# First stage of a tuned Fourier-mixing kernel by even and odd parts: 24x24 matrices on sixteen 32x32 tiles in place of 47x48 matrices on four 64x64 tiles

## The chip, the cores and the metric

The kernel runs on one core of a Trainium2 chip. A core has five engines with instruction queues of their own: TensorE (PE: matrix products; PEld is its loading of the stationary matrix), VectorE (DVE), ScalarE (ACT), GpSimd (POOL) and SyncE (SP, used here only to start DMAs). Matrix products are written to PSUM, eight banks of 2 KB for each of 128 partitions; everything else lies in SBUF. The metric is the device time of one execution in microseconds. Everything is float32.

## The reference

The input `x` has 8 batches of 3008 tokens by 256 channels. Each batch is Fourier transformed along its tokens, multiplied by a filter, and transformed back; the 24064 tokens then go through a feed-forward layer of width 2048 with a hard swish.

```python
X = np.fft.rfft(x, axis=1)
y = np.fft.irfft(X * (filt_r + 1j * filt_i)[None], n=3008, axis=1)
t = y.reshape(24064, 256)
h = t @ w_in                                  # 256 -> 2048
out = (h * np.clip(h + 3.0, 0.0, 6.0) / 6.0) @ w_out
```

## The kernel before

**The feed-forward layer** is the main loop. The 24064 tokens are 47 blocks of 512, and the 2048 hidden channels 8 parts of 256, so that there are 376 steps, block by block and part by part. Both products of a step are done with seven half-size products in place of eight (Strassen's scheme). A step's seven "up" products (A11, S1, A12, S2, S4, S3, A22; functions `up_1` to `up_5`) alternate between the two PSUM tiles `al` and `be`; its seven "down" products (`down`, numbered 1 to 7, always for the step before) go to four banks `po`. Between them ACT copies (L779, L780, L789, L808) and takes relu (L813), DVE adds (L794, L799), takes the hard swish (L818, twice a step, called half 0 and half 1 here) and makes the sums that Strassen's scheme needs (L825, L826, L831). Every float32 product is two passes over the array; a matrix with 64 output columns takes half of the array, so that `strips` sends each product as two halves that run side by side. The other inputs of a block, sums of its tokens, are made on POOL by `t_sums` (L760), once a block.

**The Fourier part** is threaded between these steps. 3008 = 47 x 64, and the transform of a batch goes in stages: the *first stage* transforms along the 47 (frequency index k, 24 of them), for each of 64 offsets c; its result goes through DRAM (`z_tmp`); the *second stage* (`b_unit`) transforms along c; then the filter (`f_unit`, `y_unit` on DVE), the way back (`bi3_unit`, result through DRAM as `g_tmp`), and last `n_five`/`n_unit`, which make the feed-forward layer's input in the ring `xn`, from which `t_sums` reads. PSUM tiles of the Fourier part are two, `psf`, used in turn by all these units; `be` is borrowed at some places.

**The first stage before.** For batches 2 to 7 (counted from 0) `a6_unit` takes 6 offsets at a time of each half of c (six units in a batch, the last with 2). For each offset it multiplies 47 rows of x by a matrix of 48 columns that holds cosines, sines and the turning factors (twiddles) of this offset; the matrices of all 32 offsets lie in `wa`. Four such products run side by side on 64x64 tiles of the array. The halves of c (h = 0, 1) land in two `psf` tiles and `be`; ACT copies one half to SBUF, and `a6_sums` on DVE makes the sum and difference of both. `z6_store` starts four DMAs from POOL's queue. A unit's x comes with four DMAs from SP (`x_load`).

**What sets the order.** Each engine's order is written out by hand: `plan` maps a step and a place in it to calls (`at`). Place 0 is after the first up products, place 1 before A22, place 2 at the end of the step. `A_AT` holds the steps of the first-stage units, counted from 7 blocks before the batch's first block; `places` those of the other stages. `late(i)` puts L831 of a step after L799 where DVE had much to do in the step before (`HEAVY`). A step that has no unit of the Fourier part is called plain below.

```python
up_1: A11 -> al, S1, A12 -> be; ACT copies al and be
do(0); DVE: hard swish half 1, L825, L826; down 1
up_2: S2 -> al, S4 -> be; DVE L794; down 2, 4
up_3: S3 -> al; DVE L799; down 5, 6; ACT relu; do(1); DVE: hard swish half 0
up_5: A22 -> al; ACT L808, relu; down 7, 3; do(2)
```

Of the kernel before, what the change touches and what calls it, by code (L numbers as in the profile page):

```python
# [10 lines left out]
FP32 = mybir.dt.float32  # L11
I32 = mybir.dt.int32
AXT = mybir.ActivationFunctionType
ALU = mybir.AluOpType
# [27 lines left out]
SIX = tuple(range(0, HC, 6))  # L42
# [36 lines left out]
def _make_tables():  # L79
# [17 lines left out]
    wf = np.zeros((P, 4, 64))  # L97
    re, im = slice(0, NC), slice(NC, P)
# [10 lines left out]
    for q in range(64):  # L109
        g, sign = (q, 1.0) if q < 32 else (31 - q, -1.0)  # L110
        co, si = (f([2 * np.pi * ((j * g) % NC) / NC for j in range(HC + 1)]) for f in (np.cos, np.sin))
        ab = np.concatenate([co, np.zeros(HC - 1) if q == 63 else si[1:HC]])
        cd, dc = ab * np.where(np.arange(NC) > HC, -1.0, 1.0), np.roll(ab, HC)
        wi[q, 3], wi[HALF + q, 3] = cd, sign * dc

        at = g % 2 * 32 + (q // 2 if q < 32 else 16 + (q - 32) // 2)
        wi[at, 0], wi[HALF + at, 0] = cd, sign * dc
        cs, sn = (np.array([f(2 * np.pi * ((j * g) % NC) / NC) for j in range(HC)]) for f in (np.cos, np.sin))
        if g % 32 == 0:
            sn = np.zeros(HC)  # L120
        for r in range(0, P, HALF):
            wf[r:r + 32, g % 2, at % 32], wf[r + 32:r + 64, g % 2, at % 32] = cs, sn
            wf[r:r + 32, g % 2, 32 + at % 32], wf[r + 32:r + 64, g % 2, 32 + at % 32] = -sign * sn, sign * cs

        for h in range(2):
            s = -1.0 if h and g % 2 else 1.0
            wf[h:HALF:2, 2, at], wf[HALF + h::2, 2, at] = s * cs, s * sn
            wf[h:HALF:2, 3, at], wf[HALF + h::2, 3, at] = -s * sign * sn, s * sign * cs
        wi[q, 1], wi[HALF + q, 1] = cd, -cd
        wi[q, 2], wi[HALF + q, 2] = sign * dc, sign * dc  # L130
# [49 lines left out]
    return wa.astype(f), wai.astype(f), wb.astype(f), wi.astype(f), wf.astype(f), start.astype(f), direct.astype(f)  # L180
# [3 lines left out]
def kernel(  # L184
# [11 lines left out]
    wa_np, wai_np, wb_np, wi_np, wf_np, start_np, direct_np = _make_tables()  # L196
# [4 lines left out]
    wf_d = nc.inline_tensor(wf_np, name="wf_t").ap()  # L201
    start_d = nc.inline_tensor(start_np, name="start_t").ap()
# [5 lines left out]

    o_d = nc.dram_tensor("o_tmp", (B * HC * NA, D), FP32, kind="Internal").ap()
# [173 lines left out]
    def x_at(b, c):  # L383
        if b == 1:
            return xs[:, (b * NB + c) % 3, :, :], c * XC, XC
        t = xs.rearrange("p i j d -> p (i j) d")
        return t[:, ds((b * len(SIX) + c) % 2 * 6, 6), :], SIX[c], min(6, HC - SIX[c])

    def x_load(b, c):
        t, c0, n_ = x_at(b, c)  # L390
        rows = x[b].rearrange("(a c) d -> a c d", c=NC)
        for h in range(2):
            for r, n in ((0, 32), (32, NA - 32)):
                nc.sync.dma_start(t[h * 64 + r:h * 64 + r + n, 0:n_, :], rows[r:r + n, ds(h * HC + c0, n_), :])

# [70 lines left out]
    def a6_unit(b, c):  # L470
        xc, c0, n = x_at(b, c)
        n //= 2
        t = t3p.tile([P, 3, 2, D], FP32, name="t3") if n == 3 else t1p.tile([P, 2, 2, D], FP32, name="t1")
        banks = [psF.tile([P, 512], FP32, name="psf", tag="f") for h in range(2)]
        be = psU.tile([P, 512], FP32, name="be") if n == 3 else None
        for r in range(n):
            for g in range(2):
                for h in range(2):
                    j, ps, o = (2, be, h) if r == 2 - 2 * h and n == 3 else (r - h if n == 3 else 0,) + (banks[h], r - h if n == 3 else 0)
                    q = g * n + j  # L480
                    nc.tensor.matmul(ps[ts(g, 64), ts(o, D)], wa[ds(h * 64, NA), ds((c0 + q) * 2 * KH, 64)],  # L481
                                     xc[ds(h * 64, NA), q, :], start=True, stop=True)
            if n == 3 and r == 0:
                nc.vector.tensor_copy(out=t[:, 2, 1, 0:2], in_=be[:, D:D + 2])
        m = min(n, 2)
        two = [ps[:, 0:m * D].rearrange("p (j d) -> p j d", d=D) for ps in banks]
        nc.scalar.activation(out=t[:, 0:m, 0, :], in_=two[0], func=AXT.Copy)
        if n == 3:
                nc.scalar.activation(out=t[:, 2, 1, 2:D], in_=be[:, D + 2:], func=AXT.Copy)
        st["t1", b, c] = t, be, two[1], n  # L490

    def a6_sums(b, c):
        t, be, ps, n = st["t1", b, c]
        v, m = nc.vector, min(n, 2)
        if n == 3:
            v.tensor_tensor(out=t[:, 2, 0, :], in0=be[:, 0:D], in1=t[:, 2, 1, :], op=ALU.add)
            v.tensor_tensor(out=t[:, 2, 1, :], in0=be[:, 0:D], in1=t[:, 2, 1, :], op=ALU.subtract)
        v.tensor_tensor(out=t[:, 0:m, 1, :], in0=t[:, 0:m, 0, :], in1=ps, op=ALU.subtract)
        v.tensor_tensor(out=t[:, 0:m, 0, :], in0=t[:, 0:m, 0, :], in1=ps, op=ALU.add)

    def z6_store(b, c):
        t, _, _, n = st.pop(("t1", b, c))
        for g in range(2):
            for ri in range(2):
                p0 = g * 64 + ri * KH
                nc.gpsimd.dma_start(z_d[b, :, ri, ds(SIX[c] + n * g, n), :, :].rearrange("k j s d -> k (j s d)"),  # L506
                                    t[p0:p0 + KH, 0:n, :, :].rearrange("p j s d -> p (j s d)"))
# [24 lines left out]
    def b_unit(b, i):  # L532
        c, r = divmod(2 * i, TC)
        if b > 1:
            t = st.pop(("t2", b, c))
            ps = [bank(b) for k in range(2)]
            for s_ in range(2):
                for ri in range(2):
                    for k in range(2):
                        nc.tensor.matmul(ps[k][ds(ri * 64 + s_ * 32, 32)].rearrange("p (v d) -> p v d", v=2),  # L540
                                         wf[ts(k, 64), s_, ts(ri, 32)], t[ts(k, 64), :, s_, :], start=True, stop=True)
            for k in range(2):
                st["ps", b, i + k] = ps[k].rearrange("p (u d) -> p u d", u=2)
            return
        ps = bank(b).rearrange("p (u d) -> p u d", u=2)
        for u in range(2):

            k, w = (r // 2 + 2 * u, wf[:, 2:4, :].rearrange("p a m -> p (a m)")) if b else (r + u, st["wb", b, c][:, r + u, :])
            (strips if b else nc.tensor.matmul)(ps[:, u, :], w, st["t2", b, c][:, k, :], start=True, stop=True)
        st["ps", b, i] = ps  # L550
# [219 lines left out]
    def up_1(k, p):  # L770
# [5 lines left out]
        product(al, p, A11, t[:, F1, :], start=True)  # L776
        product(be[:, 1, :], p, S1, xb(k, 0, 1), start=True)
# [197 lines left out]
    EARLY = (a_unit, b_unit, bi_unit, n_unit, n_five)  # L975

    def at(step, fn, *a):
        plan.setdefault((step, 0 if fn in EARLY else 1 if fn in (w_scale, bi3_unit, a6_unit) else 2), []).append((fn, a))

    with tc.manual_schedule():  # L980
# [120 lines left out]
        at(0, wai_load)  # L1101
        at(2, x_load, 1, 2)
# [37 lines left out]
        A_AT = (4, 6, 10, 12, 14, 15)  # L1140

        def places(n):
# [4 lines left out]
            a_at = [k - 7 * NP + i for i in A_AT]  # L1147
# [7 lines left out]
        for n in range(1, B):  # L1155
            a_at, f_at, y_at, bi_at = places(n)
            for c, s in enumerate(a_at):
                at(s, a_unit if n == 1 else a6_unit, n, c)
                at(s, a_sums if n == 1 else a6_sums, n, c)
                at(s, *((z_store, n, c, nc.sync) if n == 1 else (z6_store, n, c)))  # L1160
                if c >= (3 if n == 1 else 2):
                    at(max(a_at[c - 3 + (n > 1)], s - 6), x_load, n, c)
                elif n > 1:
                    at(max(prev[-1 if n == 2 else c - 2], s - 6), x_load, n, c)
            for c in range(NT):
                s = f_at[2 * (c - TB) + (n == 1)] + 1 if c >= TB else a_at[-1] + 1
                at(s, t2_load, n, c)
                s = f_at[2 * (c - FB) + 1] + 1 if c >= FB else a_at[-1 if n > 1 else 3] + 1
                at(s, table_load, n, c)
# [13 lines left out]
        HEAVY = (f_unit, y_unit, a_sums, n_five, a6_sums, bi3_unit)  # L1183

        def late(i):
            return i % NP in (1, 2) or any(fn in HEAVY for place in range(3) for fn, a in plan.get((i - 1, place), ()))

        items = [(k, p) for k in range(NBLK) for p in range(NP)]
        for i in range(len(items) + 1):
# [19 lines left out]
            up_1(k, p)  # L1209
            ends = k == LAST and p == NP - 1  # L1210
            do(0)
            last_plain = dn and kd == 0
            dn = dn and kd > 0
            if dn:
# [10 lines left out]
            if dn:  # L1225
                down(kd, pd, 2, 4)
# [26 lines left out]
            if dn:  # L1253
                if pd == NP - 1 or ends:
                    out_2(kd)
                down(kd, pd, 7, 3)
# [33 lines left out]
```

## Time and profile before

| | |
|---|---|
| median of 3 runs | 2608.41 us (2608.24 to 2608.5) |
| the profiled execution | 2608.8 us, span 2607.0 us, TensorE clock 1.0 |
| PE / PEld busy | 2591.8 us (99%) / 2051.0 us (79%) |
| DVE / ACT / POOL busy | 2053.9 us (79%) / 1295.6 us (50%) / 486.7 us (19%) |
| DMA | 200.32 MB, mean 77 GB/s |

A line of a group says: source line, engine, operation, the tile written and the tiles read, partitions x elements, how often, and then the busy time in us and the mean of one in ns. A line of the timeline says: start in us, length in us, engine, line, operation, tiles, shapes, count of merged instructions, and in square brackets the idle time of the engine ahead of it and who ended it. A float32 matrix product shows as two MATMUL instructions, one for each pass, so that the two halves of an up product are four.

### The profile page before, as it was taken

What the parts mean: (1) busy time and instruction counts of PE and PEld (TensorE: products, weight loads), DVE (VectorE), ACT (ScalarE), POOL (GpSimd) and SP (SyncE); (2) the same over time, 40 slices, a digit from 0 to 9 for tenths busy, and PEclk for the clock granted to TensorE, in tenths of its full rate; (3) what the DMA queues carried; (4) which work ended last, traced back from release to release, by engine and by line L of the source; (5) the groups of instructions that cost most, each with busy time, mean ns of one, the idle gap of its engine ahead of it and who ended that gap; (6) DMA issues with size and microseconds to landing.
All of it is one profiled execution on the core that took longest, in us unless ns stands there. A gap on an engine that the chain in (4) does not pass through costs nothing.

```text
span 2607.0 us, 86613 instructions
## 1 busy us (share of the span) xinstructions
PE 2591.8 (99%) x37708; PEld 2051.0 (79%) x37708; DVE 2053.9 (79%) x3611; ACT 1295.6 (50%) x2677; POOL 486.7 (19%) x711
## 2 busy tenths in 40 slices
PE   8999999999999999999999999999999999999999
PEld 6487777878778787788877888777877778888887
DVE  7978868888788877888778887788877888766666
ACT  4554454545545455444554444545445454455554
POOL 2242021121211202111031210311113120111110
PEclk9999999999999999999999999999999999999999
DMA  8732234112241132411224112331123321110000
GB/s 247 224 92 81 59 101 119 54 33 87 74 123 54 33 87 78 119 54 37 83 83 114 54 38 82 89 108 54 54 66 91 106 57 49 50 44 24 20 22 26
DMA packets 130834, 200.32 MB, mean 77 GB/s; under 512 B 21602, under 2 KB 97472, under 8 KB 130262
## 3 DMA queue, kind: packets, MB, share of 16 engines
q1 hardware_dynamic: 115165, 150.12, 20.4%
q0 software_dynamic: 14720, 44.16, 6.1%
q8 instruction: 296, 4.85, 0.8%
q14 instruction: 84, 0.69, 0.1%
q10 hardware_dynamic: 569, 0.50, 0.1%
HBM read 122.43 MB, written 83.98 MB: 79 GB/s over the span
## 4 chain that ended last, share of the span: by engine, by line
PE 94%; DVE 3%; DMA 2%; POOL 1%; issue 0%; ACT 0%; SPq 0%; POOLq 0%; DVEq 0%; ACTq 0%
PE po L765 43%; PE al L765 24%; PE be L765 18%; PE psn L705 2%; PE psf L540 1%; PE psf L481 1%; PE psf L600 1%; PE be L600 1%; POOL w_all L369 1%; PE be L481 1%; DVE g L818 1%; DMA g_tmp<-t 1%; PE psf L765 0%; DMA ft<-in_filt_i_dram 0%; DVE y L335 0%
## 5 line engine op out<-in xcount | busy, mean ns | idle before, releaser
L765 PEld LDWEIGHTS po<-w_all,g 128*64 128x64 f32 x20808 | 1232.5, 137 | 247.0 <-issue 12.4
L765 PE MATMUL po<-w_all,g 128*64 128x128 f32 (+1 forms) x20808 | 1407.0, 274 | 1.4 <-DVE g L818 0.7
L813 ACT ACTIVATE r<-h,half_c 128x512 f32<-128x512 f32 x736 | 531.0, 722 | 346.7 <-DVE h L794 334.7
L765 PE MATMUL al<-xt,w_all 128*64 128x256 f32 x4416 | 664.0, 379 | 0.4 <-POOL w_all L369 0.3
L818 DVE SCALAR_TENSOR_TENSOR g<-r,h 128x512 f32<-128x512 f32 x736 | 536.2, 730 | 144.6 <-ACT r L813 129.2
L765 PE MATMUL be<-xt,w_all 128*64 128x256 f32 x2944 | 442.6, 379 | 0.0
L794 DVE TENSOR_TENSOR h<-be,s 128x512 f32<-128x512 f32 x368 | 253.8, 690 | 131.3 <-PE be L765 102.2
L760 POOL TENSOR_TENSOR xt<-xn 128x256 f32<-128x256 f32 x184 | 150.7, 838 | 890.3 <-ACT xn L687 890.3
L765 PEld LDWEIGHTS be<-xt,w_all 128*64 128x64 f32 x2944 | 211.3, 137 | 106.5
L765 PEld LDWEIGHTS al<-xt,w_all 128*64 128x64 f32 x4416 | 278.9, 137 | 1.7 <-POOL w_all L369 1.4
L808 ACT ACTIVATE h<-al 128x256 f32<-128x256 f32 x368 | 141.4, 384 | 273.2 <-PE al L765 272.4
L826 DVE TENSOR_TENSOR g<-g 128x512 f32<-128x512 f32 x367 | 261.4, 712 | 12.6
L799 DVE TENSOR_TENSOR h<-al,s 128x256 f32<-128x256 f32 x368 | 156.0, 424 | 135.6 <-PE al L765 130.5
L789 ACT ACTIVATE s<-al 128x256 f32<-128x256 f32 x368 | 141.6, 385 | 207.2 <-PE al L765 207.1
L765 PE MATMUL al<-xn,w_all 128*64 128x256 f32 (+1 forms) x1536 | 240.1, 393 | 1.1 <-DVE g L818 0.7
L765 PE MATMUL be<-xn,w_all 128*64 128x256 f32 (+1 forms) x1536 | 236.4, 388 | 0.0
L780 ACT ACTIVATE s<-be 128x256 f32<-128x256 f32 x368 | 141.4, 384 | 170.1 <-PE be L765 170.1
L825 DVE TENSOR_TENSOR g<-g 128x256 f32<-128x256 f32 x367 | 165.5, 451 | 12.6
L779 ACT ACTIVATE s<-al 128x256 f32<-128x256 f32 x368 | 141.5, 384 | 59.1 <-PE al L765 59.1
L831 DVE TENSOR_TENSOR g<-g 128x256 f32<-128x256 f32 x367 | 161.7, 441 | 2.4
L765 PEld LDWEIGHTS be<-xn,w_all 128*64 128x64 f32 x1536 | 110.3, 137 | 62.3 <-issue 7.4
L506 POOL DMA_DIRECT2D z_tmp<-t x144 | 72.0, 508 | 321.4 <-ACT s L780 296.0
(162 smaller groups left out, 1766.6 us busy)
## 6 DMA issues: line engine op xcount, KB each, us to landing
t<-g_tmp SPq DMA_DIRECT2D x184, 120.0 KB
t<-z_tmp SPq DMA_DIRECT2D x42, 512.0 KB
g_tmp<-t POOLq DMA_DIRECT2D x68, 256.0 KB, 4.3
z_tmp<-t POOLq DMA_DIRECT2D x120, 144.0 KB, 3.7
o_tmp<-o SPq DMA_DIRECT2D x46, 256.0 KB
xs<-in_x_dram SPq DMA_DIRECT2D x60, 192.0 KB
ft<-in_filt_r_dram SPq DMA_DIRECT2D x168, 64.0 KB
ft<-in_filt_i_dram SPq DMA_DIRECT2D x168, 64.0 KB
```

The costliest lines, as they stand in the source:

```text
L760: nc.gpsimd.tensor_tensor(out=o, in0=x0, in1=x1, op=op_)
L765: nc.tensor.matmul(ps[ds(o, STRIP)], w[:, ds(o, STRIP)], x, skip_group_check=True, **kw)
L779: nc.scalar.activation(out=s[:, 0, :], in_=al, func=AXT.Copy)
L780: nc.scalar.activation(out=s5, in_=be[:, 1, :], func=AXT.Copy)
L789: nc.scalar.activation(out=s[:, 1, :], in_=al, func=AXT.Copy)
L794: nc.vector.tensor_tensor(out=st["h"][0].rearrange("p (a n) -> p a n", a=2), in0=be, in1=s, op=ALU.add)
L799: nc.vector.tensor_tensor(out=st["h"][1][:, 256:512], in0=al, in1=s5, op=ALU.add)
L813: nc.scalar.activation(out=r, in_=st["h"][i], func=AXT.Relu, bias=half_c, scale=1.0 / 6.0)
L818: nc.vector.scalar_tensor_tensor(out=st["g", k, p][:, o:o + 2, :].rearrange("p a n -> p (a n)"), in0=st["r", i], scalar=1.0, in1=st["h"][i ...
L825: v.tensor_tensor(out=g[:, G1, :], in0=g[:, G3, :], in1=g[:, G22, :], op=ALU.add)
L826: v.tensor_tensor(out=g[:, G3:G2 + 1:2, :], in0=g[:, G3:G1 + 1, :], in1=g[:, G11:G11 + 1, :].broadcast_to([P, 2, 256]), op=ALU.subtract)
L831: nc.vector.tensor_tensor(out=g[:, G4, :], in0=g[:, G12, :], in1=g[:, G2, :], op=ALU.subtract)
```

## The change

The first stage of batches 2 to 7 uses that the cosines are even and the sines odd in the row index. Rows a and 47 - a of x (a and 46 - a in the second half of c) are first added and subtracted; then the real part needs only the sums and a 24x24 matrix of cosines, the imaginary part only the differences and a 24x24 matrix of sines, and both matrices are the same for all offsets. The twiddles go into the matrices of the second stage.

- **Sums on POOL.** `eo_back` copies rows 46 to 24 of a batch in reverse order from DRAM to DRAM (1.5 MB, one DMA on SP). `eo_load` loads, for a unit of 16 offsets, rows 0 to 23 and the reversed rows, each to four groups of partitions, with eight DMAs on SP. `eo_sums` makes sum and difference with two POOL instructions on 128 x 1024 elements. There are four units in a batch, so 24 in all.
- **`quad_unit`** sends 32 products of 24x32 by 256 columns: for each n the 16 of (g, e, r), on sixteen 32x32 tiles of the array. The four row groups r write to four PSUM tiles: `al`, a `psf`, `be`, a `psf`. ACT copies `al` and `be`; `quad_sums` on DVE makes sums and differences of 128 x 512 elements (four instructions); `quad_store` starts eight DMAs on POOL's queue.
- **Its place** is a new one, 3, between down 7 and down 3. `quad_sums` and `quad_store` come at the end of the next step. Since the unit uses `al` and `be`, the next step's order changes: down 1 goes ahead of A11, and DVE's half-1 hard swish with its sums and down 2 go between A11 and S1.
- **The second stage** of these batches sends 16 products of 256 columns where it sent 8 of 512, each with a matrix of its own (`wb2`, 12 matrices of 128x128, loaded over `wa` at step 20).
- The steps of the units are `QUAD_AT`: in most batches 1, 4, 9, 13, where `A_AT` had 4, 6, 10, 12, 14, 15.

```diff
-        A_AT = (4, 6, 10, 12, 14, 15)
+            QUAD_AT = (3, 6, 9, 13), (1, 4, 9, 13)
...
+    def eo_back(b):
+        half = NC * D // 2
+        nc.sync.dma_start(raw(back_d[b], 0, [[half, 2], [NC * D, AH - 1], [1, half]]),
+                          raw(x[b], (NA - 1) * NC, [[half, 2], [-NC * D, AH - 1], [1, half]]))
+
+    def eo_load(b, u):
+        for r in range(4):
+            h = r % 2
+            j = h * HC + 8 * u + r // 2 * 4
+            nc.sync.dma_start(xs[ds(32 * r, AH), 0, :, :].rearrange("p j d -> p (j d)"),
+                              raw(x[b], j, [[NC * D, AH], [1, XC * D]]))
+            nc.sync.dma_start(xs[ds(32 * r + 1 - h, AH - 1), 1, :, :].rearrange("p j d -> p (j d)"),
+                              raw(back_d[b], j, [[NC * D, AH - 1], [1, XC * D]]))
+
+    def eo_sums():
+        add, back, even = (xs[:, i, :, :] for i in range(3))
+        nc.gpsimd.tensor_tensor(out=even, in0=add, in1=back, op=ALU.add)
+        nc.gpsimd.tensor_tensor(out=add, in0=add, in1=back, op=ALU.subtract)
...
+    def quad_unit(b, u):
+        banks = [psU.tile([P, 512], FP32, name="al"), psF.tile([P, 512], FP32, name="psf", tag="f"),
+                 psU.tile([P, 512], FP32, name="be"), psF.tile([P, 512], FP32, name="psf", tag="f")]
+        for n in range(2):
+            for g in range(2):
+                for e in range(2):
+                    for r in range(4):
+                        nc.tensor.matmul(banks[r][ds(64 * g + 32 * e, 32), ts(n, D)], wf[ds(32 * r, AH), 0, ts(e, 32)],
+                                         xs[ds(32 * r, AH), 2 - 2 * e, 2 * g + n, :], start=True, stop=True)
+        ts_ = [t1p.tile([P, 2, 2, D], FP32, name="t1") for w in range(2)]
+        banks = [ps.rearrange("p (n d) -> p n d", n=2) for ps in banks]
+        for w in range(2):
+            nc.scalar.activation(out=ts_[w][:, :, 0, :], in_=banks[2 * w], func=AXT.Copy)
+        st["quad", b, u] = ts_, banks[1::2]
+
+    def quad_sums(b, u):
+        for t, ps in zip(*st["quad", b, u]):
+            nc.vector.tensor_tensor(out=t[:, :, 1, :], in0=t[:, :, 0, :], in1=ps, op=ALU.subtract)
+            nc.vector.tensor_tensor(out=t[:, :, 0, :], in0=t[:, :, 0, :], in1=ps, op=ALU.add)
...
-            for s_ in range(2):
-                for ri in range(2):
-                    for k in range(2):
-                        nc.tensor.matmul(ps[k][ds(ri * 64 + s_ * 32, 32)].rearrange("p (v d) -> p v d", v=2),
-                                         wf[ts(k, 64), s_, ts(ri, 32)], t[ts(k, 64), :, s_, :], start=True, stop=True)
+            for v in range(2):
+                for s_ in range(2):
+                    for ri in range(2):
+                        for k in range(2):
+                            nc.tensor.matmul(ps[k][ds(ri * 64 + s_ * 32, 32), ts(v, D)],
+                                             wa[ts(k, 64), ds((2 * c + v) * P + s_ * 64 + ri * 32, 32)],
+                                             t[ts(k, 64), v, s_, :], start=True, stop=True)
...
+                before = a_at[c - 1] + 1 if c else max(prev[-1] + 1, s - 8)
+                if c == 0:
+                    at(before - 6, eo_back, n)
+                at(before, eo_load, n, c)
+                at(before + (c == 0), eo_sums)
+                at(s, quad_unit, n, c)
+                at(s + 1, quad_sums, n, c)
+                at(s + 1, quad_store, n, c)
...
+            def between():
+                g_sums(kd, pd)
+                if not late(i):
+                    g_last(kd, pd)
+                down(kd, pd, 2)
+
+            if after:
+                down(kd, pd, 1)
+                up_1(k, p, between)
+            else:
+                up_1(k, p)
...
-                down(kd, pd, 7, 3)
+                down(kd, pd, 7)
+                do(3)
+                down(kd, pd, 3)
```

## The prediction, made before the result was known

> **What bounds the kernel now.** I read the first part of the page, then its chain, then one unit of the old first stage with its neighbours on the timeline, and last the rows in which POOL and DVE work together.
>
> ```profile
> PE 2591.8 (99%) x37708; PEld 2051.0 (79%) x37708; DVE 2053.9 (79%) x3611; ACT 1295.6 (50%) x2677; POOL 486.7 (19%) x711
> ...
> PE 94%; DVE 3%; DMA 2%; POOL 1%; issue 0%; ACT 0%; SPq 0%; POOLq 0%; DVEq 0%; ACTq 0%
> ```
>
> TensorE is busy 99% of the span and 94% of the chain. The chain gives no time to other waits in the loop, so TensorE time taken out comes out of the span, and a new wait of TensorE goes in whole. DVE is the next engine (79%).
>
> ```profile
> 650.75 0.60 PE L765 MATMUL al<-xt,w_all 128*64 128x256 f32 x4
> ...
> 655.63 0.43 PE L481 MATMUL psf<-xs,wa 47*64 47x256 f32 x1
> ...
> 657.16 0.65 PE L765 MATMUL al<-xn,w_all 128*64 128x256 f32 x4
> ...
> 657.86 0.38 ACT L808 ACTIVATE h<-al 128x256 f32<-128x256 f32 x1 [0.20 <-PE al L765]
> ...
> 658.52 0.60 PE L765 MATMUL al<-xt,w_all 128*64 128x256 f32 x4
> ...
> 660.03 0.38 ACT L780 ACTIVATE s<-be 128x256 f32<-128x256 f32 x1 [0.48 <-PE be L765]
> ...
> 663.29 0.60 PE L765 MATMUL al<-xn,w_all 128*64 128x256 f32 x4
> ...
> 663.94 0.38 ACT L808 ACTIVATE h<-al 128x256 f32<-128x256 f32 x1 [0.89 <-PE al L765]
> ...
> 664.60 0.60 PE L765 MATMUL al<-xt,w_all 128*64 128x256 f32 x4
> ```
>
> A step runs from one A11 (al from xt after A22) to the next. The step from 658.52 to 664.60 is plain: 6.08. That from 650.75 to 658.52 holds a full unit of the old first stage (L481, before A22 at 657.16) and takes 7.77, so a unit costs 1.69.
>
> ```profile
> 749.54 1.17 POOL L760 TENSOR_TENSOR xt<-xn 128x256 f32<-128x256 f32 x1
> ...
> 750.80 1.07 POOL L760 TENSOR_TENSOR xt<-xt 128x256 f32<-128x256 f32 x1
> ...
> 751.30 0.84 DVE L825 TENSOR_TENSOR g<-g 128x256 f32<-128x256 f32 x1
> 751.82 0.91 POOL L922 TENSOR_TENSOR o<-p,o 128x256 f32<-128x256 f32 x1
> ...
> 752.18 1.10 DVE L826 TENSOR_TENSOR g<-g 128x512 f32<-128x512 f32 x1
> ```
>
> Here POOL and DVE hold each other up. L760 takes 0.73 in the median, L825 0.42, L826 0.69; beside each other 1.17, 0.84 and 1.10. L818 (0.69 alone) ran from 750.05 to 751.27. Had the two shared evenly, it would have ended near 751.0; that it ended 0.56 after L760's end at 750.71 says one waits for the other's whole instruction. Rows that read PSUM (L561, at most 0.693 in 84 cases) are never stretched.
>
> **The change part by part.** The sum is made against the profiled execution's 2608.8, 0.4 over the median.
>
> *Old units removed.* A batch has five full units (+1.69 each) and one of two offsets (its step is 6.82, so +0.74): 9.19 a batch, 55.1 in six batches. Their sums, copies and DMAs go too; TensorE waited for none, so these give nothing.
>
> *quad_unit on TensorE.* 32 float32 products are 64 passes on 16 tiles, four passes deep. A pass of 256 columns is 0.2135 of streaming (an up product of four takes 0.43 of PE for two pairs: 658.52 to 658.95). Sixteen products of `b_unit` (L540), on tiles of 64x32, start 7 ns apart. Four passes (0.85), 16 starts (0.11) and fill (0.12) make 1.08. The nearest row, the old unit, held TensorE 1.53 (655.63 to 657.16). Floor: 0.85 (streaming alone); ceiling: 1.93 (half rate, passes of 0.427, if four tile rows that write four banks could not run together). I take 1.08, as nothing in L540's rows halves.
>
> The unit starts only when ACT has copied A22 out of `al`: L808 ends 1.03 after A22's start (663.29, 663.94 + 0.38), and with 0.06 to pass on, 1.09; down 7 ends at 0.87. So 0.22 of idling and 1.1: +1.32 a step, x 24 = 31.7. Rows of ACT (50% busy) give no gain here.
>
> The Trainium skill, "TensorE: Matmul & The Clock Gate", section "Wait — 56ns, not 53.3ns?", speaks against this: starts of products never lie closer than about 25 ns, however small they are. By it the 64 passes of a unit would take an estimated 1.6, and the total would be 12.5 higher. The row beside it, L540 with 7 ns between starts, differs, as its products go to different tiles, and the row decides.
>
> *The step after a unit.* Down 1 no longer stands between A12 and S4; S4 overwrites `be`, which L780 copies until 0.65 + 0.385 after A12's start (A12 ran from 659.38, L780 from 660.03). S4 would come 0.87 after A12 (A12 and S2, 0.43 each), now at 1.10 (with 0.06 to pass on): +0.23, x 24 = 5.5. Down 1 itself has its input from the step before. Floor 0, if S1's and down 2's places cover it; ceiling 0.48, ACT's idle ahead of L780.
>
> *Second stage.* 36 units send 16 products of 256 columns for 8 of 512: the same columns streamed; 16 more starts of 7 ns less what overlaps, 0.02 each: 0.7 in all (0 to 4). `wb2` (786 KB) comes at step 20, long before use.
>
> *quad_sums on DVE.* Four instructions of 0.68 each, as L561's 128x512 sums from PSUM: 2.7, against 2.2 for an old full unit (0.42, 0.42, 0.68, 0.69 at 657.70 to 659.90), but per batch 10.9 against about 12: no more load. They come at the end of the next step and so the second `psf` tile comes free about 2.1 into the step after. Behind it stand `n_five` (five batches, step after the second unit), waiting about 0.73, or two `n_units` (four batches, 0.62); elsewhere the half-1 hswish comes late and down 2 waits 0.22 to 0.38. Counted over the 24 units: 11.3. Floor 0 (DVE's 21% idle takes it); ceiling 24 x 0.73 = 17.5.
>
> *eo_sums on POOL: the largest term.* L369's 128 columns take 0.46, L760's 256 take 0.73: 0.19 + 2.1 ns a column, so 1024 columns take an estimated 2.36. Each of the 48 can hold up DVE's instructions with two SBUF inputs (L818, L825, L826, L831) by all but its first 0.19: 2.2. POOL first issues the eight DMAs of `quad_store` (0.507 each, L506: 4.05), so the sums start 5 us into the second step after the unit. Walk through one unit, times from that step's A11: hold 1 from 5.1 to 7.3; L831, due at 5.9, ends at 7.7; down 3, due at 7.0, starts at 7.77: 0.76 lost. Hold 2 from 7.4 (POOL had waited for L831) to 9.9; half 0 of the hard swish, due 7.75, ends 10.6; down 1 of the next step, due 9.5, starts at 10.64: 1.13 lost, in all 1.9. The same walk gives 2.0 for a batch's first unit, 1.8 for the third and 2.8 for the last, whose second hold meets half 1 too; 8.5 a batch, 6.6 in the first of the six, whose steps are others: 5 x 8.5 + 6.6 = 49. Floor 0 (DVE's slack takes every hold; a gain is excluded, as POOL did not make these sums before); ceiling 48 x 2.2 = 106 (each hold reaches TensorE whole). I take 49, from the rows of 749 to 752, the only ones in which the two engines meet in a train.
>
> The Trainium skill, "SBUF — State Buffer", section "Who interferes with whom", gives the same pair a lock held for the whole instruction: the loser waits it out and does not share. By it the term is 49; by even sharing, as a rival below has it, about 20. The trace agrees at 0.73 us instructions; none of 2.4 us is in it.
>
> *DMAs.* `eo_load`'s eight DMAs (for four of `x_load`) go through SP's queue in 0.3 to 0.7 each, three steps (18 us) ahead; what stands behind them there are loads with more than a step to spare. `eo_back` (1.5 MB, 1 KB pieces) starts six steps, 36 us, ahead of the first `eo_load`; if it ran on two DMA engines only it would take about that. POOL's queue: eight starts in place of four, at 19% busy; `t_sums` stands behind `eo_sums` once a block, and has about 1 us to spare, counted above for the third unit. I cost all of this at nothing; if the reversed rows came late, the sums would be late, and a unit would wait with all of TensorE behind it.
>
> Sum: 2608.8 - 55.1 + 31.7 + 5.5 + 0.7 + 11.3 + 49 = 2651.9; against the median, **2651**.
>
> **The rivals.**
> - *DVE and POOL share more finely.* Each instruction of DVE is then only stretched, by 1.75 (L818 1.22 for 0.69), while POOL's sum lasts, and the loss per hold is 0.35 to 0.5 in place of 0.95 to 1.4: 0.7 to 1.0 a unit, 17 to 24. Against it: 751.27. Total 2619 to 2626.
> - *Faster: POOL's sums fall into DVE's idle time.* For it: DVE idles 21%, and down 3 has room before L831 is needed. Then the total is 2608.8 - 55.1 + 31.7 + 5.5 + 0.7 + 11.3 = 2603, and 2591 if DVE's backlog costs nothing either. It decides from a POOL term under 6 us, 0.25 a unit; I counted 1.9 for the unit walked. Against it: L818 and L831 stand one instruction ahead of what TensorE wants.
> - *The sixteen tiles run at half rate.* 0.85 more a unit: 24 x 0.85 = 20.4, total 2672. Against it: L540's starts.
> - *Between:* a POOL term of 1 to 11 us, total 2603 to 2614.
>
> **How the numbers follow.** The forecast has 0.52, with its own range of 2635 to 2666 (POOL term 33 to 64); finer sharing 0.20 (up to 2635); faster 0.14; between 0.08; half rate or a late `eo_back` 0.06. About 0.2%, 5.2 us, is what a measurement can tell from no change: faster is under 2603.2, slower over 2613.6. The range leaves out the faster case and the half rate: 2603 to 2668. Slower is 0.52 + 0.20 + 0.06 = 0.78.
>
> **What the changed kernel's profile would show.** The unit step is 7.4 long; quad_unit holds TensorE 1.08 and starts 0.06 after L808 (half rate: 1.9). In the next step S4 waits for L780. POOL's sums of 128x1024 show 2.4 or more, and L818, L826, L831 of up to 2.9 beside them; TensorE's waits on L831 and L818 add up to some 49. If those DVE rows are long but the steps are not, the walk is wrong; if they stay near 1.2, the finer sharing is right. `n_five` after a batch's second unit starts late, ended by `quad_sums`. A wait of POOL's sums on `xs` would show `eo_back` late.
>
> What would make it wrong: sums that start earlier or later by 1 us meet other DVE instructions, and the walk gives another loss; and a stall that takes the place of another counts once.

## The result, and the profile after

The changed kernel takes 2842.2 us (2836.03 to 2848.3), the one before 2608.32: a ratio of 1.0897 (95% interval 1.0874 to 1.0921), 234 us slower. The prediction had the direction right and the size far off: +43, and a range that ended at 2668.

The page after (span 2846.5 us), its busy times, the clock granted to TensorE in 40 slices, and the chain that ended last by engine and by line. After's lines stand about 16 further down than before's: L781 is the old L765, L835 the old L818, L776 `t_sums`, L503 `quad_unit`, L423 and L424 `eo_sums`, L694 the load for `n_five`.

```profile
PE 2661.0 (93%) x39052; PEld 2090.7 (73%) x39052; DVE 2103.4 (74%) x3545; ACT 1294.6 (45%) x2659; POOL 631.5 (22%) x808
...
PEclk9999989999899998999989999899998999999999
...
PE 76%; DMA 12%; POOL 4%; DVE 4%; issue 2%; SPq 1%; ACT 1%; POOLq 0%; DVEq 0%; ACTq 0%
PE po L781 34%; PE al L781 19%; PE be L781 14%; DMA xs<-back_tmp 9%; PE psn L721 2%; POOL xs L423 1%; POOL xs L424 1%; PE psf L555 1%; DMA out_dram<-o 1%; POOL xt L776 1%; DVE g L835 1%; DMA t<-g_tmp 1%; PE psf L616 1%; PE al L503 1%; PE be L616 1%
```

Before, the chain was TensorE for 94% and no DMA of the loop was on it. Now `xs<-back_tmp`, the load of the reversed rows, has 9% of it, 256 us; in six slices the mean clock is under 0.9 of full speed. TensorE stands idle 2846.5 - 2661.0 = 185.5 us (15 before). The same from TensorE's own waits (what it waited for, us in total, times, longest):

```profile
PE al L503 <- POOL xs L423: 88.0, 12, 12.0
PE al L781 <- POOL xt L776: 24.4, 10, 5.1
PE al L503 <- POOL xs L424: 18.3, 12, 2.1
PE psn L721 <- DMA t<-g_tmp: 9.1, 2, 8.3
```

Twelve of the 24 units wait for their sums, and `t_sums`, which stands in POOL's queue behind late sums, is then late too (the second line). One of the twelve units, on the timeline (start, length, engine, line):

```profile
701.32 0.61 PE L781 MATMUL po<-w_all,g 128*64 128x128 f32 x8
...
709.51 2.34 POOL L423 TENSOR_TENSOR xs<-xs 128x1024 f32<-128x1024 f32 x1 [15.53 <-DMA xs<-back_tmp]
711.93 2.34 POOL L424 TENSOR_TENSOR xs<-xs 128x1024 f32<-128x1024 f32 x1
...
711.90 0.63 PE L503 MATMUL al<-xs,wf 24*32 24x256 f32 x1 [9.97 <-POOL xs L423]
```

TensorE ends down 7 at 701.93 and stands for 9.97; POOL stood for 15.53, for the reversed rows. The unit's products then take 0.63 where they take 0.4 at full clock. The windows of this stretch (us, the busy time of PE, PEld, DVE, ACT, POOL, granted clock, busy share of the 16 DMA engines, GB/s):

```profile
680.00:704.00 24.00, 21.42 (x340) 16.88 (x336) 15.77 (x29) 11.85 (x26) 4.00 (x8) 1.00 0.37 112
704.00:716.00 12.00, 2.75 (x63) 1.17 (x64) 1.01 (x2) 0.00 (x0) 4.68 (x2) 0.58 0.14 46
716.00:726.00 10.00, 9.95 (x127) 7.44 (x104) 3.45 (x6) 4.46 (x9) 0.07 (x1) 0.82 0.19 59
```

The clock falls to a half at 706.0, 4.1 us after the last product, and stays there for 13.65 us, well into the work that follows. So a wait of this length is paid twice. Shorter ones can be paid so too: at 634.33 the clock fell after 1.35 us of a gap.

And why the rows are late, from two windows in which little else was on the DMA engines:

```profile
282.00:289.00 7.00, 7.00 (x100) 5.84 (x98) 5.63 (x10) 3.37 (x7) 0.00 (x0) 1.00 0.06 26
618.00:623.00 5.00, 5.00 (x72) 4.09 (x70) 4.07 (x6) 2.49 (x5) 4.77 (x7) 1.00 0.06 26
```

A DMA share of 0.06 is one engine of 16. The rows of `back_tmp` are then moving, packets of 4 KB in single file, 0.159 us each: 23 of them are 3.7 us, and the four loads of a unit an estimated 14.6 us in a row. Measured from the first load's issue to the start of the first sum, it is 18 us where little else moves (611.38 to 629.51), and 22 to 27 us in the twelve units that wait (684.53 to 709.51 in the one shown), whose packets share the engine with other transfers. The loads of 24 rows of x in the same unit bring the packets under way at once to 12 or 13. Behind these loads, in the same queue, stood `n_five`'s (L694, 8.3 us of waiting once).

### The profile page after: what moved, and what is told of

Same layout as the page of the kernel before. It is cut to its first block, busy times and chain, and to the rows that moved or that the text cites. A ratio compares the mean times of both kernels' runs of the same rounds, so it can differ in the third digit from the quotient of the medians.

```text
span 2846.5 us, 89392 instructions
## 1 busy us (share of the span) xinstructions
PE 2661.0 (93%) x39052; PEld 2090.7 (73%) x39052; DVE 2103.4 (74%) x3545; ACT 1294.6 (45%) x2659; POOL 631.5 (22%) x808
## 4 chain that ended last, share of the span: by engine, by line
PE 76%; DMA 12%; POOL 4%; DVE 4%; issue 2%; SPq 1%; ACT 1%; POOLq 0%; DVEq 0%; ACTq 0%
PE po L781 34%; PE al L781 19%; PE be L781 14%; DMA xs<-back_tmp 9%; PE psn L721 2%; POOL xs L423 1%; POOL xs L424 1%; PE psf L555 1%; DMA out_dram<-o 1%; POOL xt L776 1%; DVE g L835 1%; DMA t<-g_tmp 1%; PE psf L616 1%; PE al L503 1%; PE be L616 1%
## 5 line engine op out<-in xcount | busy, mean ns | idle before, releaser
L781 PE MATMUL po<-w_all,g 128*64 128x128 f32 (+1 forms) x20808 | 1437.2, 278 | 16.2 <-DVE g L835 8.6
L781 PEld LDWEIGHTS po<-w_all,g 128*64 128x64 f32 x20808 | 1250.3, 139 | 275.1 <-issue 29.4
L781 PE MATMUL al<-xt,w_all 128*64 128x256 f32 x4416 | 675.6, 385 | 24.5 <-POOL xt L776 24.4
L835 DVE SCALAR_TENSOR_TENSOR g<-r,h 128x512 f32<-128x512 f32 x736 | 546.3, 744 | 157.4 <-ACT r L830 140.4
L781 PE MATMUL be<-xt,w_all 128*64 128x256 f32 x2944 | 449.2, 384 | 6.5 <-POOL xt L776 5.2
L776 POOL TENSOR_TENSOR xt<-xn 128x256 f32<-128x256 f32 x184 | 151.4, 842 | 832.8 <-ACT xn L703 832.8
L781 PEld LDWEIGHTS al<-xt,w_all 128*64 128x64 f32 x4416 | 283.4, 139 | 32.3 <-POOL xt L776 27.6
L781 PEld LDWEIGHTS be<-xt,w_all 128*64 128x64 f32 x2944 | 210.2, 138 | 125.9 <-ACT s L797 12.2
L843 DVE TENSOR_TENSOR g<-g 128x512 f32<-128x512 f32 x367 | 276.1, 752 | 12.6
L825 ACT ACTIVATE h<-al 128x256 f32<-128x256 f32 x368 | 141.5, 384 | 293.1 <-PE al L781 291.3
L781 PE MATMUL al<-xn,w_all 128*64 128x256 f32 (+1 forms) x1536 | 239.3, 392 | 1.4 <-DVE g L835 0.7
L781 PE MATMUL be<-xn,w_all 128*64 128x256 f32 (+1 forms) x1536 | 239.4, 392 | 0.3 <-DVE t L627 0.3
L842 DVE TENSOR_TENSOR g<-g 128x256 f32<-128x256 f32 x367 | 178.5, 487 | 12.6
L848 DVE TENSOR_TENSOR g<-g 128x256 f32<-128x256 f32 x367 | 176.2, 480 | 2.4
L503 PE MATMUL al<-xs,wf 24*32 24x256 f32 x384 | 56.1, 502 | 107.4 <-POOL xs L423 88.0
L781 PEld LDWEIGHTS be<-xn,w_all 128*64 128x64 f32 x1536 | 110.6, 139 | 60.6 <-issue 8.9
```

Source lines behind the costliest of these rows:

```text
L776: nc.gpsimd.tensor_tensor(out=o, in0=x0, in1=x1, op=op_)
L781: nc.tensor.matmul(ps[ds(o, STRIP)], w[:, ds(o, STRIP)], x, skip_group_check=True, **kw)
L835: nc.vector.scalar_tensor_tensor(out=st["g", k, p][:, o:o + 2, :].rearrange("p a n -> p (a n)"), in0=st["r", i], scalar=1.0, in1=st["h"][i ...
L842: v.tensor_tensor(out=g[:, G1, :], in0=g[:, G3, :], in1=g[:, G22, :], op=ALU.add)
L843: v.tensor_tensor(out=g[:, G3:G2 + 1:2, :], in0=g[:, G3:G1 + 1, :], in1=g[:, G11:G11 + 1, :].broadcast_to([P, 2, 256]), op=ALU.subtract)
L848: nc.vector.tensor_tensor(out=g[:, G4, :], in0=g[:, G12, :], in1=g[:, G2, :], op=ALU.subtract)
```

## The experiments

Line numbers in the variants are up to nine higher than in the changed kernel. Times are medians; each was timed beside the kernel before on its chip (2608.0 to 2608.7).

**1. m1_loads, m2_back, m3_both: the loads, the copy, both.**

```diff
# m1_loads, in eo_load
-            nc.sync.dma_start(xs[ds(32 * r + 1 - h, AH - 1), 1, :, :].rearrange("p j d -> p (j d)"),
-                              raw(back_d[b], j, [[NC * D, AH - 1], [1, XC * D]]))
+            for o, m in ((0, 16), (16, AH - 17)):
+                nc.sync.dma_start(xs[ds(32 * r + 1 - h + o, m), 1, :, :].rearrange("p j d -> p (j d)"),
+                                  raw(back_d[b], j + o * NC, [[NC * D, m], [1, XC * D]]))
# m2_back, in eo_back
-        half = NC * D // 2
-        nc.sync.dma_start(raw(back_d[b], 0, [[half, 2], [NC * D, AH - 1], [1, half]]),
-                          raw(x[b], (NA - 1) * NC, [[half, 2], [-NC * D, AH - 1], [1, half]]))
+        part = NC * D // 16
+        nc.sync.dma_start(raw(back_d[b], 0, [[part, 16], [NC * D, AH - 1], [1, part]]),
+                          raw(x[b], (NA - 1) * NC, [[part, 16], [-NC * D, AH - 1], [1, part]]))
```

> Edit: each load of the 23 reversed rows is split into one of 16 and one of 7 rows; the copy eo_back stays as it is. Theory A: in the changed kernel each of these loads runs on one DMA engine only (packets of 4 KB one after another, 0.159 each: 23 x 0.159 = 3.7, four in a row 14.6 a unit), the sums on POOL come late, TensorE stands still before the unit and then has half its clock for some 10 us. By A the unit's wait goes at all but the first unit of a batch (whose load follows the end of eo_back at once), half-clock stretches disappear nearly all, and the time is 2600 to 2670. Rival B: eo_back, 46 pieces of 32 KB on two engines (29.5 us), is what comes late: then the time stays above 2790.

> Edit: eo_back in 16 parts of 4 KB pieces in place of two parts of 32 KB pieces; the loads of 23 rows stay. By A only the wait of a batch's first unit shrinks (about 6 us in five batches, with its half-clock stretch about 10): 2790 to 2842. By B about 2651, or 2603 to 2651.

> Edit: both, loads of 16 and 7 rows and eo_back in 16 parts. By A and B no unit waits for its rows and the clock stays at 1.0; what is left is the rest of the prediction's sum: 2651 if POOL's sums lock DVE as walked, 2619 to 2626 if the two share more finely, 2603 or less if the sums fall into DVE's idle time. Rival C (the sums are late because they stand behind other work in POOL's queue, or the loads behind other transfers): stays above 2750.

Measured: m1_loads 2674.2 (two runs), m2_back 2836.1 (two runs), m3_both 2672.3 (ratio 1.0246, 1.0229 to 1.0263). The loads alone account for 168 us of the 234; the copy, although it ran some 29 us on two engines, for 6 by the medians, which is no more than the changed kernel's own runs lie apart (2836.0 to 2848.3). Rivals B and C fall. In m3_both TensorE idles 2668.3 - 2603.6 = 64.7 us against 185.5, and is busy 2603.6 against 2661.0. So of the 178 us between the two profiled executions 121 were standing still and 57 the same products taking longer. That fits the clock: products recorded at half clock fill 134.8 us after and 12.9 in m3_both, and half of the difference is 61.

**2. m14_22: 22 rows and 1 in place of 16 and 7.** To see why 23 rows stay on one engine.

```diff
-            for o, m in ((0, 16), (16, AH - 17)):
+            for o, m in ((0, AH - 2), (AH - 2, 1)):
```

> Edit: the changed kernel with each load of 23 reversed rows split into one of 22 rows and one of 1 row, in place of 16 and 7. Theory: the rows are dealt out over as many DMA engines as the largest divisor of their number up to 16; 22 rows go to 11 engines (two packets of 0.159 each), the time is as m1_loads, 2665 to 2685. Rival: a number over 16 that is no multiple of 8 stays on one engine: 22 x 0.159 = 3.5 a load, 14 a unit, and the time stays above 2800.

Measured: 2672.0 (two runs), as with 16 and 7. So 22 rows spread and 23 do not, and the multiple of 8 is not the reason. The Trainium skill, "DMA: Bandwidth & Descriptors", section "Why a DMA increments its semaphore by 16 and not by 1", says how the number of engines is chosen: the largest number up to 16 that divides the slowest dimension of both sides. The runs agree in all that they show: 23 rows on one engine, the copy with an outer dimension of 2 on two, 22 spread. I had not drawn on this page; it gives this change's largest term.

**3. m4_nosums: what POOL's sums cost.** The unit's products read the loaded rows, not their sums and differences, so the first stage of batches 2 to 7 is not the transform here.

```diff
-                                         xs[ds(32 * r, AH), 2 - 2 * e, 2 * g + n, :], start=True, stop=True)
+                                         xs[ds(32 * r, AH), 1 - e, 2 * g + n, :], start=True, stop=True)
...
-                at(before + (c == 0), eo_sums)
```

> Edit: as m3_both, and eo_sums is left out: the unit's products read the loaded rows themselves in place of their sums and differences, all products, loads, copies and stores being the same in number and size (so the first stage of batches 2 to 7 is not the transform). m3_both less this one is the price of POOL's sums: 49 by the lock, 17 to 24 by finer sharing, under 6 if DVE's idle time takes them. This one itself: 2603 by the terms for the unit (+1.32), the step after (+0.23) and DVE's backlog (11.3 in all); 2591 if the backlog costs nothing.

Measured: 2620.3 (1.0045; 1.003 to 1.006), 52.0 below m3_both. In m4_nosums the unit holds TensorE longer than in m3_both (1.72 against 1.42 to 1.49; its products read another third of the same tile on the same partitions, and why that is slower stays open), about 0.25 a unit, 6 in all. So the sums cost about 58, some 6 of it by the clock (two half-clock stretches of 6.8 us in m3_both, none in m4_nosums but at the end). How, on the timeline of m3_both (L844 is the old L826, L849 the old L831, L817 the old L799):

```profile
728.44 2.39 POOL L424 TENSOR_TENSOR xs<-xs 128x1024 f32<-128x1024 f32 x1 [2.75 <-PE be L782]
730.90 2.69 POOL L425 TENSOR_TENSOR xs<-xs 128x1024 f32<-128x1024 f32 x1
```

```profile
728.64 2.73 DVE L844 TENSOR_TENSOR g<-g 128x512 f32<-128x512 f32 x1
731.41 2.46 DVE L849 TENSOR_TENSOR g<-g 128x256 f32<-128x256 f32 x1
733.79 0.68 DVE L812 TENSOR_TENSOR h<-be,s 128x512 f32<-128x512 f32 x1
734.39 0.41 DVE L817 TENSOR_TENSOR h<-al,s 128x256 f32<-128x256 f32 x1
```

```profile
734.85 0.65 PE L782 MATMUL al<-xn,w_all 128*64 128x256 f32 x4 [1.51 <-DVE h L817]
```

L844 takes 2.73 for 0.69 and L849 2.46 for 0.42: each is held up by 2.04. For the first that is POOL's 2.39 less 0.35; the second POOL sum is itself stretched, 2.69 against the 2.34 that it took in the changed kernel with DVE idle. Other DVE instructions with two SBUF inputs that start under a sum also last until about its end, the late starters for 1.0 to 1.7 us. The sums that read PSUM (L812, L817) keep 0.68 and 0.41, and none of the 368 of each takes more than 0.70 and 0.43. A22 then stands 1.51 for L817. Even sharing would by an estimate (twice their length) have stretched the two DVE instructions to about 1.4 and 0.8. This is the lock that the prediction read from the train at 749 to 752, now with 2.4 us instructions.

**4. m7_wide: 16 products of 512 columns.**

```diff
-        for n in range(2):
-            for g in range(2):
-                for e in range(2):
-                    for r in range(4):
-                        nc.tensor.matmul(banks[r][ds(64 * g + 32 * e, 32), ts(n, D)], wf[ds(32 * r, AH), 0, ts(e, 32)],
-                                         xs[ds(32 * r, AH), 2 - 2 * e, 2 * g + n, :], start=True, stop=True)
+        for g in range(2):
+            for e in range(2):
+                for r in range(4):
+                    nc.tensor.matmul(banks[r][ds(64 * g + 32 * e, 32)].rearrange("p (n d) -> p n d", n=2),
+                                     wf[ds(32 * r, AH), 0, ts(e, 32)],
+                                     xs[ds(32 * r, AH), 2 - 2 * e, 2 * g:2 * g + 2, :], start=True, stop=True)
```

> Edit: as m3_both, but quad_unit sends 16 products of 512 columns in place of 32 of 256. In m3_both the unit holds TensorE 1.42 to 1.49 and its 64 passes start 19 ns apart. Theory: the starts set that time (64 x 19 to 22 ns and the last pass); with 32 passes of 0.427 in two layers it falls to 1.05 or so, the sum is 24 x 0.4 = 10 less: 2662. Rival: the four banks or the sixteen tiles slow the streaming itself: then the unit keeps 1.45 and the time stays at 2672.

Measured: 2663.2 (1.0211; 1.0195 to 1.0226), 9.1 less than m3_both. The unit now holds TensorE 1.08 to 1.24 in most cases (1.07 in m11_after and m12_early). So neither the banks nor the number of tiles slows the streaming: the number of starts sets the time. They lie 18 to 19 ns apart only in the mean. In m3_both the first half of a unit's starts comes in bursts, 7 ns apart, with pauses of 0.1 to 0.2 us, and the second half comes at a steady 16 to 17 ns. What holds them apart stays open.

**5. m5_split: the sums in eight parts.**

```diff
-        nc.gpsimd.tensor_tensor(out=even, in0=add, in1=back, op=ALU.add)
-        nc.gpsimd.tensor_tensor(out=add, in0=add, in1=back, op=ALU.subtract)
+        for j in range(XC):
+            nc.gpsimd.tensor_tensor(out=even[:, j, :], in0=add[:, j, :], in1=back[:, j, :], op=ALU.add)
+            nc.gpsimd.tensor_tensor(out=add[:, j, :], in0=add[:, j, :], in1=back[:, j, :], op=ALU.subtract)
```

> Edit: as m3_both, but POOL's two sums of 128x1024 are eight of 128x256 (0.73 each, as L760). Lock by single instructions: a hold is 0.53 in place of 2.1 to 2.2, DVE gets in between, and most of a hold falls into the 1 us that DVE idles in a step: 0.1 (as the sums of a block in the kernel before, a step of 7.66 for 7.54) to 0.8 a unit, 3 to 19 in all in place of 52, so 2622 to 2640. Rival: what counts is the whole time for which POOL holds the pair (8 x 0.53 = 4.2, as 2 x 2.1): then it stays at 2672 or grows.

Measured: 2651.5 (1.0165; 1.015 to 1.0181), 20.8 less: between theory and rival. Most steps that meet the parts now lose nothing. What is left sits in three kinds of step: one with `y_unit`, 9.42 for 7.74; the first step of a block, 9.2 to 10.6 for 6.08, where `t_sums` stands behind the third unit's sums; and the second unit's step, 8.8 to 10.8 for about 8.4.

**6. m8_all: the three together,** and down 4 ahead of S4 in the step after a unit.

> Edit: m5_split and m7_wide together, and in the step after a unit down 4 goes ahead of S4, so that S4 no longer stands 0.23 idle for L780's copy. If all three prices add: 2672 - (32 to 50) - 10 - 5 = 2607 to 2625. Under 2603 only if DVE's backlog after quad_sums costs nothing either.

Measured: 2653.6 (1.0172; 1.0155 to 1.0189), no better than m5_split, so the expectation failed: the prices do not add. The unit's step got shorter (8.06 for 8.36), the next too (5.75 to 5.80 for 5.91), but the one after longer (6.57 for 6.25): DVE, late after `quad_sums`, gives most of the 0.45 back. And the waits for `t_sums` and for the second unit's rows were the same or worse (up to 12.1).

**7. m9_order, m10_s4, m11_after: the order.** m9_order keeps the split sums and wide products and moves three things; m10_s4 adds down 4 ahead of S4; m11_after puts the unit behind down 3.

```diff
# m9_order: quad_sums first in the next step; sums of units 1 and 3 moved
-    EARLY = (a_unit, b_unit, bi_unit, n_unit, n_five, eo_load)
+    EARLY = (a_unit, b_unit, bi_unit, n_unit, n_five, eo_load, quad_sums)
-        HEAVY = (f_unit, y_unit, a_sums, n_five, quad_sums, bi3_unit)
+        HEAVY = (f_unit, y_unit, a_sums, n_five, bi3_unit)
-                at(before + (c == 0), eo_sums)
+                at(max(before + 1, s - 4) if c == 0 else s - 2 if c == 2 else before, eo_sums)
# m11_after
-                down(kd, pd, 7)
-                do(3)
-                down(kd, pd, 3)
+                down(kd, pd, 7, 3)
+                do(3)
```

> Edit: m5_split and m7_wide together (sums in eight parts, products of 512 columns), and three moves: quad_sums at place 0 of the step after the unit, where DVE was idle for 3.2 us in m4_nosums, in place of its end; the first unit's sums four steps ahead of the unit, away from y_unit; the third unit's sums two steps ahead of the unit, behind t_sums. Theory: m8_all did not gain what its parts gained because DVE, late after quad_sums, took the gain back in the next step (6.57), and because POOL's sums held up t_sums (a block's first step of 9.2 to 12.1 for 6.08) and a step with y_unit (9.63 for 7.96). Then a unit's three steps take 7.95 + 5.91 + 6.08, 1.7 over plain, 41 in all, and 2608 - 55 + 41 and some 10 for sums that still meet DVE: 2600 to 2610. Rival: the order is not the reason, and the sums cost the same wherever they lie: 2645 to 2655.

> Edit: m9_order with down 4 ahead of S4 in the step after a unit. With DVE no longer late there, S4's 0.23 of standing idle goes: 5.5 less than m9_order, 2595 to 2605. Rival: DVE's sum of be (L794 of the kernel before) then comes as late as it did and gives the time back: no difference.

> Edit: m10_s4, and the unit stands behind down 3 in place of ahead of it, with down 1 and 2 both between the unit and A11. The unit then no longer waits 0.22 for L808's copy of A22, and 0.87 of down products cover ACT's copy of the unit's al (0.6): 5.3 less than m10_s4, 2590 to 2600. Rival: the wait only moves to A11 or S1, which wait for ACT's two copies (0.6 each): no difference.

Measured: 2636.1 (1.0106; 1.0091 to 1.0121), 2634.8 (1.0104; 1.0088 to 1.0119), 2633.3 (1.0099; 1.0082 to 1.0116). The order was worth 17 over m8_all, a third of what theory had; the two smaller moves cannot be told from nothing in the total. In the steps the three moves did what they were made for: a unit's three steps take 8.2, 5.4 and 6.08 in m11_after where no sums meet them, 1.3 to 1.5 over plain. One step takes it all back: the second unit of a batch, 11.2 to 14.4, which stands only three steps after the first, while its rows can be loaded only once the first has been read.

**8. m12_early and m13_dve.**

```diff
# m12_early
-            QUAD_AT = (3, 6, 9, 13), (1, 4, 9, 13)
+            QUAD_AT = (3, 6, 9, 13), (-1, 4, 9, 13)
# m13_dve, besides; i from 0 to 3, called two a step
+    def eo_sums(i):
+        add, back, even = (xs[:, a, 2 * (i // 2):2 * (i // 2) + 2, :] for a in range(3))
+        if i % 2 == 0:
+            nc.vector.tensor_tensor(out=even, in0=add, in1=back, op=ALU.add)
+        else:
+            nc.vector.tensor_tensor(out=add, in0=add, in1=back, op=ALU.subtract)
```

> Edit: m11_after with the first unit of batches 3 to 7 two steps earlier (steps -1, 4, 9, 13 in place of 1, 4, 9, 13). In m11_after the second unit's step takes 11.2 to 14.8 where the others take 8.1 to 8.4, as it follows three steps after the first and its rows and sums need longer. Theory: with five steps between them that goes, 3 to 6 in each of the batches: 2607 to 2617. Rival: the time is lost to POOL's sums wherever the unit lies: stays above 2625.

> Edit: m12_early with the sums on DVE in place of POOL, four instructions of 128x512 a unit, at the ends of the two steps ahead of the unit (where two units lie three steps apart, in the step ahead and in the unit's own). DVE idles 0.8 to 1.1 there until ACT has the relu. If the lock between POOL and DVE is what the sums cost, the 2.8 of DVE's own time a unit costs TensorE 0 to 0.6 a unit, and with 2608 - 55 + 24 x 1.3 (what a unit's three steps take over plain in m11_after) the time is 2584 to 2600. Rival: DVE is as full as POOL's lock made it, and the sums cost as much there: 2610 or more.

Measured: m12_early 2611.2 (1.0015; 1.0005 to 1.0025), as theory had it: the second unit's step is 8.3. It is the best version found and still 0.15% behind the kernel before. m13_dve 2628.4 (1.008; 1.0065 to 1.0095), on the rival's side but mostly not for the rival's reason: the last unit's rows, asked for one step after the third unit, had not landed when DVE's queue came to its sums, and DVE stood with all of the layer behind it (steps of 9.3 to 15.0 for 7.5 in four of six batches, which is all that m13_dve loses to m12_early). Work that waits for a transfer is worse placed on the fuller queue. Where the rows were there, the sums cost 1.2 at a batch's first unit, nothing at the second and 0.7 at the third on DVE, and 0.75, nothing and 0.6 on POOL in m12_early. So DVE was no cheaper, and in this the rival was right.

**9. m16_gate: the sums spread by hand.**

```diff
+        if gate:
+            nc.gpsimd.tensor_copy(out=gate_t, in_=st["g_now"][:, 0, 0:1])
...
+                    parts = (2, 2, 2, 2) if c == 0 else (2, 3, 3) if s - before > 3 else (4, 4)
+                    for i, m in enumerate(parts):
+                        at(s - len(parts) + i - (c == 0), eo_sums, sum(parts[:i]), sum(parts[:i + 1]), True)
```

> Edit: m12_early with POOL's eight sums of a unit spread over three or four steps (2 to 4 in each): ahead of each group POOL copies one column of the step's hard swish, so that the group starts when DVE has done half 0 and idles until the next relu. Theory: a step loses time only where so many of DVE's instructions meet a hold that its idle 1.1 is used up (A22 then waits for L799's sum, 18 times some 0.6 in m12_early); with two or three sums a step this goes: 2598 to 2606. Rival: the whole time of the holds counts: 2608 to 2616, as m12_early, or more by the copies.

Measured: 2626.1 (1.0067; 1.005 to 1.0084), outside both. TensorE's waits in m12_early and then in m16_gate:

```profile
PE al L783 <- DVE h L819: 10.6, 18, 1.8
```

```profile
PE al L510 <- POOL xs L430: 7.1, 3, 4.2
...
PE al L789 <- DVE h L825: 1.2, 3, 0.6
```

The waits of A22 for DVE (L819 and L825 are the old L799) fell from 10.6 to 1.2 as theory said. But the last unit's sums, four in each of the two steps ahead of it, now came too late (7.1, and steps of 1.7 to 7.4 more). Nor did the rest gain what the waits lost: away from the last units m16_gate is only about 1 us shorter than m12_early, as other steps grew (the third unit's by 0.4). That spreading pays is not shown; no run has it together with sums in time.

## Why the prediction was wrong

**The step that failed** is the one on DMAs: "`eo_load`'s eight DMAs ... go through SP's queue in 0.3 to 0.7 each, three steps (18 us) ahead", and "I cost all of this at nothing". It priced the issue of the loads, and took the transfer as hidden because it began 18 us ahead. The four loads of 23 rows share one engine, 14.6 us by the packets alone, and the rows were there 18 us after the first issue at best and 22 to 27 in the twelve units that waited. TensorE was ready for these units 15 to 25 us after that issue, and POOL's first sum (2.4) still stood ahead of them; the other twelve had 32 to 70 us and waited for nothing. The mechanism was in reach: for `eo_back` the prediction itself reckoned with two DMA engines, from the same kind of access pattern, and was not far off its length (36 against some 29 measured); it did not ask the same of the loads, which matter more (m1_loads against m2_back). Its case "late `eo_back`" had 0.06 together with another, with no price of its own. The whole term was 170 us (2842.2 less m3_both), of which about a third is the half clock after each long idle, which the prediction left out.

The other steps, from the runs without that term:

- *Old units removed, -55.1.* Confirmed in the steps: where a unit was, the step is shorter by 1.69 or 0.74.
- *quad_unit 1.08, +1.32 a step.* Mis-sized: 1.42 to 1.49 in 21 of m3_both's 24 units, 0.34 to 0.41 more, 8 to 10 in all. L540 was misread: its 16 starts are two bursts of eight, 7 ns apart, with 0.41 us between the bursts, and I took the 7 ns for a rate that 64 can keep; the mean was 18 to 19 ns in m3_both and 22 in m4_nosums. The rule of the Trainium skill that I set aside ("TensorE: Matmul & The Clock Gate", section "Wait — 56ns, not 53.3ns?", no starts closer than about 25 ns) gave an estimate of 1.6, closer than my row did. As a floor it does not agree with these traces, whose starts lie 7 and 16 to 17 ns apart. That m3_both's 2672 equals the total of the rival with half rate is chance: that unit would have held TensorE 1.9, and 16 products of 512 columns took 1.08. The 0.22 ahead of the unit and the start right after the copy of A22 were as said.
- *The step after, 0.23.* Right: in m4_nosums A12 starts at 698.95 and S4 at 700.04, 1.09 later. The price is small and, with DVE late, could not be had back (m8_all).
- *Second stage, 0.7.* Nothing: the unit holds TensorE 1.02 before and after.
- *DVE's backlog, 11.3.* Right in kind, somewhat high. In m4_nosums the step after next is 0.16 longer, 0.54 with the `n_units` and 0.70 with `n_five` in it, about 8 in all.
- *eo_sums, 49.* Right in mechanism, a little low: 58 by m4_nosums, of which some 6 are a lower clock that comes of it. The waits on the old L831 and L818 add up to 20.4 in m3_both, not to 49; 18 more stand on two other DVE instructions behind them (12.2 on the old L799, 5.8 on the old L826). The rivals of finer sharing and of "the idle time takes it" fall by the rows of 728 to 733. What the walk could not give is where the loss falls when the sums move, as m9_order and m12_early show.

Without the 23-row loads, then, the sum stands at 2651 against 2672 measured, +43 against +64, outside its case's own range of 2635 to 2666: the unit's length and the POOL term were both some 9 too low and the backlog some 3 too high. The remaining 6 are not placed. The signs to look for did their work: "a wait of POOL's sums on `xs`" was listed as a sign, though put down to the wrong DMA.

## What to carry to other kernels

Price a moved or added load by its transfer, not only by its issue: from its row count and the trace, how many of the 16 engines will it use? 23 rows took an estimated 14.6 us of packets in four loads; with 16 + 7 the units waited once, for 1.9 us, and with 22 + 1 never. Work added on POOL that reads SBUF is added on DVE's instructions with two SBUF inputs as well: short instructions in steps with idle DVE time, not two long ones. And in a kernel that keeps TensorE 99% busy, a small gain in products is soon spent: in m12_early TensorE is busy 12.9 us less than before (2578.9 against 2591.8) and idle 14.8 more (30.0 against 15.2), and the change about breaks even.

## What the runs showed of the hardware that was not expected

- Loads of 23 rows from DRAM run on one DMA engine (share 0.06, 26 GB/s, packets of 4 KB every 0.159 us); 16, 7, 22 and 24 rows spread.
- In the case shown TensorE's clock was halved after 4.1 us of idling, for 13.65 us. Most other stretches lasted 6.8 to 13.7 (3.4 to 17 in all), some after shorter gaps: in m3_both gaps of 2.06 and 2.76 us were followed by one, and one of 2.12 was not. Some 57 us of the slowdown are products at that clock.
- 64 passes of 256 columns on sixteen 32x32 tiles start 18 to 19 ns apart in the mean (bursts at 7 ns with pauses, then a steady 16 to 17), 22 ns when another third of the same SBUF tile is read; with 512 columns in place of 256 the same unit takes 1.07 to 1.24 in place of 1.42 to 1.49.
- A POOL instruction of 2.4 us held up a DVE instruction with two SBUF inputs that started just after it by 2.04 us, until about its own end, and left those that read PSUM alone.
